# Masks in four row tiles of 32, one transpose for the one-hots of both sides, and later sequences' rows in the MLP's memory

## The chip, the cores and the metric

The kernel runs on one core of one Trainium2 chip. A core has TensorE (matrix products, out of SBUF into PSUM), VectorE, ScalarE and GpSimd (element-wise work), and SyncE, which here issues most of the DMAs. Each engine works through its own list of instructions in order and waits for others by semaphores. The metric is the device time of one execution in microseconds, as the median of several runs.

## What is computed

The kernel joins a clustered attention and an MLP with a layer norm in front. Queries and keys are each assigned to the centroid that they are most similar to; a query attends only to keys of its own cluster.

```
B, H, S, D = 4, 8, 768, 64;  16 centroids per head
q_assign = argmax(q_n @ c_n^T);  k_assign = argmax(k_n @ c_n^T)
mask   = q_assign[:, None] == k_assign[None, :]
attn   = softmax(where(mask, q k^T / 8, -1e9));  a = attn @ v        # per batch and head
x      = a of all heads side by side                                 # (4, 768, 512)
xn     = (x - mean) / sqrt(var + 1e-6) * g
out    = x + relu(xn @ w1) @ w2                                      # w1 512x2048, w2 2048x512
```

## The kernel before

**Pairs, steps, units.** Two heads of one sequence make a pair; there are 16 pairs, four to a sequence (b). Head j of a pair lies in partitions 64j to 64j+63. A step `(n, g, c)` is pair n, half g of its queries (384 columns), block c of its keys (128), for both heads, so a pair has 12 steps. The main loop (L565) takes two steps per turn: a turn is called a unit here, and `slot` 0 to 5 counts the six units of a pair. 

**Scores.** `scores(i)` (L321) fills the PSUM tile `s_ps` of step i (two banks, one per head; two such tiles exist) and takes its exponential. For each head there is first a mask product and then the product of keys and queries, accumulated on it. The mask product multiplies one-hot rows of the queries' clusters (bf16, tile `m` of side 0) with the keys' one-hot rows, turned into 0 for a hit and -2^100 for a miss (`m` of side 1); one head's one-hots fill 16 of its 64 rows, the others are zero. Both products work on 64 rows, head 0 in the upper half of the array and head 1 in the lower (L339). ScalarE then writes `e = exp(s/8)` (L332), with five buffers.

**Weighing.** `weigh(i)` (L344) multiplies `e` with v into `a_ps` (L351; one buffer; each head takes 64 columns of the array) and lets VectorE add up the `e` of a half (L365, L368) for the denominators. After six blocks ScalarE copies the accumulator out (L377).

**Preparing the next pair.** During pair n the next one is prepared, spread over the slots: q and k are transposed on TensorE (`prep_transpose`, L237, k in slot 0 and q of the pair after in slot 5), similarities with the centroids (`prep_sims`, slot 1), their transposes and the maximum (`prep_turn`, `prep_route`, slot 2), and in slot 4 `prep_onehot` (L291): for each side six transposes of one-hots (two heads x 64 columns to 128 rows) into a PSUM tile `oh_ps`, and one ScalarE operation from there into `m`: a copy for the queries (L307), an Identity with bias and scale for the keys (L305). `finish` (L381) computes the denominators of the last pair (slot 1), their reciprocals (slot 3), and scales and stores x (slot 5), once transposed to `xT_d` and once by rows to `x_d`. VectorE also turns the weights, which arrive as float64, into float32 (`split_weight`, `join_weight`).

**The norm.** For a sequence b, `rows_load` (L444) brings rows of x back (tile `xr`, two buffers, from the pool `small`, which lives through the whole kernel), `norm_rows` takes their statistics (`bn_stats`, L455), `norm_stats` (L458) takes the root on ScalarE (L462, with a load of another function table, and the table of the exponential is loaded again at its next use), and `norm_stat_rows` and `norm_apply` spread and apply them.

**The MLP.** After the attention, its pools are closed (L625) and `hid` and `ffn` are opened in their memory. Both layers use a scheme of seven block products instead of eight (`first_layer`, `second_layer`), with sums of operands made by VectorE and copies out of PSUM by ScalarE.

**What sets the order.** In the attention (L547) TensorE, VectorE and ScalarE follow the order that the code writes. In the MLP (L784) only TensorE does; the others, and SyncE throughout, are put in order by a planner, which may place work as soon as its data and memory allow by its own reckoning. The norm of sequence 0 is written into the attention (L529 to L540). That of the others is written into the MLP's loop (L810 to L835), but the planner placed the rows and the statistics of sequences 1 and 2 earlier: the roots (L462) of the four sequences ran at 231.65, 269.82, 353.29 and 506.42 us of the span, and the attention ends near 395.

**The start.** Pair 0's q is loaded in four DMAs on SyncE's queue and its k in four on ScalarE's, behind the centroids (L88, L102). Its products of the first two steps run ahead of the masks, which are then added on top.

Of the kernel before, what the change touches and what calls it, by code (L numbers as in the profile page):

```python
# [19 lines left out]
def kernel(  # L20
# [24 lines left out]
    SCALE = 1.0 / D ** 0.5  # L45
    FAR = 2.0 ** 100
# [5 lines left out]
    small = ctx.enter_context(tc.tile_pool(name="small", bufs=2))  # L52
# [17 lines left out]
    def ps(name, dt=F32, n=512):  # L70
        return pools["t"].tile([P, n], dt, tag="t", name=name)
# [4 lines left out]
    def load(n, names):  # L76
        if n >= len(pairs):
            return
        b, pr = pairs[n]
        for name in names:  # L80

            shape = [P, 2, NT, D] if name == "v" else [P, NT, 2, D]
            t = loads.tile(
                shape, F32, tag=name, name=f"{name}_sb", bufs=2 if name == "v" else 1
            )

            parts = 1 if n or name == "v" else NHALF
            queue = nc.sync if n or name != "k" else nc.scalar  # L88
            for g in range(parts):
                cs = slice(g * NT // parts, (g + 1) * NT // parts)  # L90
                for j in range(2):
                    queue.dma_start(
                        out=t[:, j] if name == "v" else t[:, cs, j, :],
                        in_={"q": q, "k": k, "v": v}[name][b, 2 * pr + j].rearrange(
                            "(p c) d -> p c d", p=P
                        )[:, cs, :],
                    )
            loaded[n][name] = t


    c_sb = const.tile([H * NCL, D], F32, name="c_sb")
    nc.scalar.dma_start(out=c_sb, in_=centroids.rearrange("h c d -> (h c) d"))  # L102
    load(0, "qkv")

    ident = const.tile([P, P], F32, name="ident")
    make_identity(nc, ident)
    identb = const.tile([P, P], BF16, name="identb")
# [6 lines left out]
    eps = const.tile([P, 1], F32, name="eps")  # L114
    nc.gpsimd.memset(eps, 1e-6)

    onehot = route.tile([P, TH, 2, NHALF, 2, D], BF16, name="onehot")
    nc.gpsimd.memset(onehot, 0.0)
    NG = TH * 2 * NHALF * 2
    hits = const.tile([P, B * NPAIR], F32, name="hits")  # L120
    far = const.tile([P, 1], F32, name="far")
    nc.gpsimd.memset(far, -FAR)
# [124 lines left out]
    def prep_sims(n):  # L247

        _, pr = pairs[n]
        sim = ps("sim_ps")  # L250
        for side in range(2):
            for g in range(NHALF):
                r = (side * NHALF + g) * Q
                nc.tensor.matmul(  # L254
                    sim[r : r + Q, :HC],
                    cT[:, pr, :, :].rearrange("p j c -> p (j c)"),
                    prepared[n][side][:, g * HC : (g + 1) * HC],
                    start=True,
                    stop=True,
                    tile_position=(0, r),  # L260
                )
        sim_sb = route.tile([P, HC], F32, tag="sim", name="sim_sb")
        nc.scalar.copy(sim_sb, sim[:, :HC])
        prepared[n]["sim"] = sim_sb
# [10 lines left out]
    def prep_route(n):  # L275
        simT = prepared[n]["simT"]
        sims = simT[:, :HC].rearrange("p (g c) -> p g c", c=NCL)
        best = route.tile([P, NG], F32, tag="best", name="best")
        nc.vector.tensor_reduce(best, sims, AX.X, ALU.max)

        nc.vector.scalar_tensor_tensor(
            out=onehot.rearrange("p c s g j d -> p (c s g j) d")[:, :, :NCL],
            in0=sims,
            scalar=1.0,
            in1=best.unsqueeze(2).to_broadcast([P, NG, NCL]),
            op0=ALU.mult,
            op1=ALU.is_equal,
            accum_out=hits[:, n : n + 1],
        )

    def prep_onehot(n):  # L291
        for side in range(2):
            t = ps("oh_ps", BF16, 1024)
            for g in range(NHALF):
                for c in range(TH):
                    o = (g * TH + c) * P
                    nc.tensor.transpose(  # L297
                        t[:, o : o + P],
                        onehot[:, c, side, g, :, :].rearrange("p j d -> p (j d)"),
                        identb,  # L300
                    )
            m = heads.tile([P, S], BF16, tag=f"m{side}", name=f"m{side}")

            if side:
                nc.scalar.activation(m, t[:, :S], AF.Identity, bias=far, scale=FAR)  # L305
            else:
                nc.scalar.copy(m, t[:, :S])  # L307
            prepared[n]["m", side] = m

# [1 line left out]

    x_d = [spill.tile([NT, P, DM], F32, name=f"x_d{b}") for b in range(B)]
    xs = {}
    soft = {}
    sums = {}
    accs = {}
    late = {}

    def scores(i, first="mask", parts=("mask", "qk", "exp")):  # L321
        n, g, c = steps[i]
        st = prepared[n]
        if parts[0] == first:
            st["s", i] = ps_s.tile([P, 2, 512], F32, tag="s", name="s_ps")
        s = st["s", i]
        keys, cols = slice(c * P, (c + 1) * P), slice(g * HC, (g + 1) * HC)
        rows = [slice(j * D, (j + 1) * D) for j in range(2)]
        for part in parts:
            if part == "exp":  # L330
                e = attn.tile([P, 2, HC], F32, tag="e", name="e", bufs=5)
                nc.scalar.activation(e, s[:, :, :HC], AF.Exp, scale=SCALE)  # L332
                soft[i] = e
                continue
            of_keys, of_queries = {
                "mask": lambda: (st["m", 1], st["m", 0]), "qk": lambda: (st[1], st[0])
            }[part]()
            for j in range(2):
                nc.tensor.matmul(  # L339
                    s[:, j, :HC], of_keys[rows[j], keys], of_queries[rows[j], cols],  # L340
                    start=part == first, stop=part != first, skip_group_check=True,
                )

    def weigh(i):  # L344
        n, g, c = steps[i]
# [97 lines left out]

    def rows_load(b, t):  # L444
        if t < NT:
            x = small.tile([P, DM], F32, tag="xr", name="xr")
            nc.sync.dma_start(out=x, in_=x_d[b][t])
            rows[b, t] = x

# [97 lines left out]
    with tc.manual_schedule(engines=order):  # L547
        prep_transpose(0, 0)
        load(1, "q")
        turn_centroids()  # L550
        prep_transpose(0, 1)
        load(1, "k")
        prep_sims(0)
        scores(0, "qk", ("qk",))
        prep_turn(0)
        scores(1, "qk", ("qk",))
        prep_route(0)
        prep_transpose(1, 0)
        load(2, "q")
        load_weight(0)  # L560
        load_weight(1)
        prep_onehot(0)
        scores(0, "qk", ("mask", "exp"))
        scores(1, "qk", ("mask", "exp"))
        for u in range(len(pairs) * slots):  # L565
            n, slot = divmod(u, slots)
            nxt = n + 1 < len(pairs)
            if slot == 1:
                load(n + 1, "v")
            if slot == 0 and nxt:  # L570
                prep_transpose(n + 1, 1)
                load(n + 2, "k")
            if slot == 1 and nxt:
                prep_sims(n + 1)
            if slot == 2 and nxt:
                prep_turn(n + 1)
                prep_route(n + 1)
            if slot == 4 and nxt:
                prep_onehot(n + 1)
            if slot == 5 and n + 2 < len(pairs):  # L580
                prep_transpose(n + 2, 0)
                load(n + 3, "q")
            if slot == 1 and n:
                finish(n - 1, 0)
            for i in (2 * u + 2, 2 * u + 3):
                if i < len(steps):
                    scores(i)
            weigh(2 * u)
            weigh(2 * u + 1)
            if slot == 3 and n:  # L590
                finish(n - 1, 1)
            if slot == 5 and n:
                finish(n - 1, 2)
            m = 2 * n + slot // 3
            if slot % 3 == 0:
                split_weight(m)
            elif slot % 3 == 1:
                join_weight(m)
                load_weight(m + 2)
            for job in extra.pop((n, slot), ()):  # L600
                job()
# [434 lines left out]
```

## Time and profile before

| | us |
|---|---|
| median of 4 runs (982.78 to 987.36) | 983.2 |
| profiled execution, whole time | 985.0 |
| profiled execution, span from first to last instruction | 983.2 |
| attention, to the last weighing's end | about 395 |
| MLP | about 588 |
| TensorE matmul busy | 961.6 |
| VectorE busy | 642.5 |
| ScalarE busy | 307.7 |

How to read the profile's lines. A group line names the source line, the engine, the operation, what it writes and reads, the tile of TensorE's array that it uses (rows*columns), partitions x elements and type, then the count, the busy time in total, the mean time of one in ns, and the engine's idle time just before with what ended it. A line of the timeline begins with the start and the length of a merged group in us; a bracket gives the idle time before it and what ended that. A line of the waits gives the total, the number and the longest. Matmuls are pipelined: the lengths of two that follow each other overlap, so what an instruction costs on the path is read from one start to the next. A float32 product appears as two passes, each with a record of its own.

### The profile page before, as it was taken

How to read it: one execution, taken by the hardware profiler on the slowest of the kernel's cores; microseconds unless marked ns; L12 is line 12 of the kernel's file. 1: busy time of each engine (PE TensorE's matmuls, PEld its weight loads, DVE VectorE, ACT ScalarE, POOL GpSimd, SP SyncE). 2: the span in 40 equal slices, each digit the busy share in tenths (PEclk: the TensorE clock that was granted, in tenths of full speed). 3: DMA queues.
4: the chain of work that ended last, by engine and by line, in shares of the span. 5: the costliest groups of instructions: out<-in, count | busy, mean ns of one | idle time of the engine just before them, and what ended most of it. 6: DMA issues, size and time to landing. Idle time of an engine off the chain costs nothing.

```text
span 983.2 us, 12870 instructions
## 1 busy us (share of the span) xinstructions
PE 961.6 (98%) x4854; PEld 596.3 (61%) x4854; DVE 642.5 (65%) x1206; ACT 307.7 (31%) x497; POOL 2.8 (0%) x27
## 2 busy tenths in 40 slices
PE   6999999999989989999999999999999999999997
PEld 3444444444444434555888656888556888556886
DVE  3888888998889989776645355654455654455431
ACT  4656666667566655221000121000221000221000
POOL 1000000000000000000000000000000000000000
PEclk9999999999999989999999999999999999999999
DMA  6356666666755643220212000211000212000011
GB/s 173 92 140 168 176 172 164 163 166 170 198 134 142 179 132 87 71 80 17 92 54 71 10 1 1 97 60 64 6 1 0 97 60 70 1 0 6 28 41 37
DMA packets 141444, 84.01 MB, mean 85 GB/s; under 512 B 110608, under 2 KB 127040, under 8 KB 141376
## 3 DMA queue, kind: packets, MB, share of 16 engines
q1 hardware_dynamic: 139104, 82.70, 30.2%
q8 instruction: 40, 0.66, 0.3%
q10 hardware_dynamic: 2272, 0.43, 0.2%
q14 instruction: 28, 0.23, 0.1%
HBM read 64.00 MB, written 19.00 MB: 84 GB/s over the span
## 4 chain that ended last, share of the span: by engine, by line
PE 91%; DVE 5%; DMA 1%; ACT 1%; issue 1%; SPq 0%; ACTq 0%; DVEq 0%
PE x_ps L719 17%; PE x_ps L634 17%; PE s_ps L339 14%; PE a_ps L351 12%; PE z_ps L719 8%; PE z_ps L634 8%; PE y_ps L719 4%; PE y_ps L634 4%; PE qk_ps L237 2%; DVE es L368 2%; PE sim_ps L254 1%; PE den_ps L388 1%; PE oh_ps L297 1%; DVE bn L455 1%; PE simT_ps L270 1%; DMA q_sb<-in_q_dram 1%
## 5 line engine op out<-in xcount | busy, mean ns | idle before, releaser
L332 ACT ACTIVATE e<-s_ps 128x768 f32<-128x768 f32 x192 | 151.6, 813 | 61.1 <-PE s_ps L339 59.4
L339 PE MATMUL s_ps<-t,t 64*128 64x384 f32 x768 | 156.4, 486 | 0.0
L351 PE MATMUL a_ps<-e,v_sb 128*64 128x384 f32 x768 | 146.9, 505 | 3.0 <-ACT x L377 3.0
L368 DVE TENSOR_TENSOR es<-es,e 128x768 f32<-128x768 f32 x128 | 122.1, 954 | 12.1 <-ACT e L332 5.9
L351 PEld LDWEIGHTS a_ps<-e,v_sb 128*64 128x64 f32 x768 | 47.2, 137 | 91.0 <-issue 87.2
L719 PE MATMUL x_ps<-w2t,h 128*128 128x256 f32 x384 | 84.5, 379 | 0.0
L339 PEld LDWEIGHTS s_ps<-t,t 64*128 64x128 f32 x768 | 69.3, 191 | 22.4 <-issue 22.4
L719 PEld LDWEIGHTS x_ps<-w2t,h 128*128 128x128 f32 x384 | 72.7, 190 | 10.1
L649 ACT COPY u<-x_ps 128x384 f32<-128x384 f32 x64 | 30.7, 479 | 135.4 <-PE x_ps L634 135.4
L339 PE MATMUL s_ps<-m,m 64*128 64x384 bf16 x384 | 63.8, 329 | 3.8 <-ACT e L332 2.4
L521 DVE TENSOR_TENSOR ws<-w 128x256 f32<-128x256 f32 x64 | 24.9, 420 | 60.8 <-PE z_ps L634 60.8
L649 ACT COPY p<-x_ps 128x384 f32<-128x384 f32 x32 | 15.3, 479 | 139.9 <-PE x_ps L634 139.0
L730 DVE TENSOR_TENSOR o_sb<-x_ps,xb 128x256 f32<-128x256 f32 x48 | 20.2, 421 | 57.7 <-PE x_ps L719 57.7
L654 DVE TENSOR_TENSOR h<-z_ps,u 128x384 f32<-128x384 f32 x64 | 35.3, 552 | 25.8 <-ACT u L649 14.4
L339 PEld LDWEIGHTS <-m 64*128 64x128 bf16 x384 | 18.7, 93 | 48.2 <-issue 31.2
L634 PE MATMUL x_ps<-xt,ws 128*128 128x384 f32 x128 | 46.6, 487 | 0.9 <-DVE ws L521 0.9
L634 PE MATMUL x_ps<-xn,w 128*128 128x384 f32 x128 | 46.6, 487 | 0.6 <-ACT late L377 0.6
L634 PE MATMUL z_ps<-xt,ws 128*128 128x384 f32 x128 | 46.6, 487 | 0.0
L634 PE MATMUL x_ps<-xt,w 128*128 128x384 f32 x128 | 46.6, 487 | 0.0
L634 PE MATMUL x_ps<-xn,ws 128*128 128x384 f32 x128 | 46.5, 486 | 0.0
L634 PE MATMUL y_ps<-xn,w 128*128 128x384 f32 x128 | 46.5, 486 | 0.0
L634 PE MATMUL z_ps<-xn,ws 128*128 128x384 f32 x128 | 46.5, 486 | 0.0
(122 smaller groups left out, 1296.1 us busy)
## 6 DMA issues: line engine op xcount, KB each, us to landing
raw<-in_moe_w_ch_dram SPq DMA_DIRECT2D x32, 512.0 KB, 3.9
v_sb<-in_v_dram SPq DMA_DIRECT2D x32, 192.0 KB, 3.7
xn<-xT_d SPq DMA_DIRECT2D x16, 384.0 KB, 4.6
xr<-x_d SPq DMA_DIRECT2D x24, 256.0 KB, 2.9
xb<-x_d SPq DMA_DIRECT2D x48, 128.0 KB, 2.1
out_dram<-o_sb SPq DMA_DIRECT2D x48, 128.0 KB, 1.7
q_sb<-in_q_dram SPq DMA_DIRECT2D x30, 192.0 KB, 3.9
k_sb<-in_k_dram SPq DMA_DIRECT2D x30, 192.0 KB, 3.7
```

Of the source, the lines that this page charges most:

```text
L237: nc.tensor.transpose(t[:, c * P : (c + 1) * P], src[:, g * TH + c, :, :].rearrange("p h d -> p (h d)"), ident,)
L254: nc.tensor.matmul(sim[r : r + Q, :HC], cT[:, pr, :, :].rearrange("p j c -> p (j c)"), prepared[n][side][:, g * HC : (g + 1) * HC], start= ...
L332: nc.scalar.activation(e, s[:, :, :HC], AF.Exp, scale=SCALE)
L339: nc.tensor.matmul(s[:, j, :HC], of_keys[rows[j], keys], of_queries[rows[j], cols], start=part == first, stop=part != first, skip_group_ch ...
L351: nc.tensor.matmul(acc[j * D : (j + 1) * D, :HC], loaded[n]["v"][:, j, c, :], e[:, j, :], start=(c == 0), stop=(c == NT - 1),)
L368: nc.vector.tensor_tensor(es, es, soft.pop(i), ALU.add)
L521: nc.vector.tensor_tensor(t[:, i], x, y, op)
L634: nc.tensor.matmul(bank[:, :HC], lhs[:, c, :], rhs[:, c, :], start=first and c == 0, stop=c == NDH - 1, skip_group_check=True,)
L649: nc.scalar.copy(t, bank[:, :HC])
L654: nc.vector.tensor_tensor(h, bank[:, :HC], other, ALU.add)
L719: nc.tensor.matmul(bank[:, :MH], hidden[lhs + (c,)][:, tt * P : (tt + 1) * P], rhs[:, c, :], start=first and c == 0, stop=c == NFH - 1, sk ...
L730: nc.vector.tensor_tensor(o, bank[:, :MH], x, ALU.add)
```

## The change

- **Masks of a unit together.** `masks(u)` issues four mask products, for two steps and two heads, each on 32 rows at row 0, 32, 64 and 96 of the array. The keys' one-hots of even blocks lie in rows 0 to 63 and of odd blocks in rows 64 to 127 (`mk`); the queries' one-hots lie in both halves (`mq`). Then come the products and exponentials of the two steps (`products`, `exponentials`).
- **One-hots of both sides in one transpose.** A one-hot has 32 columns instead of 64, so two sides and two heads fill 128 columns, and six transposes do for what took twelve. Four ScalarE operations on 64 partitions each (two Identities over 384 elements, two copies over 768) fill `mk` and `mq` in place of two on 128 partitions over 768.
- **Rows in other memory.** `xr` comes from `last` for sequence 0, and from `ffn`, which exists only after the attention, for the others.
- **First loads.** q of pair 0 is issued ahead of the centroids, and of q and k the first head's DMAs go to SyncE's queue and the second head's to ScalarE's.

```diff
-            queue = nc.sync if n or name != "k" else nc.scalar
             for g in range(parts):
                 cs = slice(g * NT // parts, (g + 1) * NT // parts)
                 for j in range(2):
+                    queue = nc.scalar if parts > 1 and j else nc.sync
                     queue.dma_start(
...
+    load(0, "q")
     c_sb = const.tile([H * NCL, D], F32, name="c_sb")
     nc.scalar.dma_start(out=c_sb, in_=centroids.rearrange("h c d -> (h c) d"))
-    load(0, "qkv")
+    load(0, "kv")
...
-    onehot = route.tile([P, TH, 2, NHALF, 2, D], BF16, name="onehot")
+    onehot = route.tile([P, TH, NHALF, 2, 2, Q], BF16, name="onehot")
...
-                r = (side * NHALF + g) * Q
+                r = (g * 2 + side) * Q
...
     def prep_onehot(n):
-        for side in range(2):
-            t = ps("oh_ps", BF16, 1024)
-            for g in range(NHALF):
-                for c in range(TH):
-                    o = (g * TH + c) * P
-                    nc.tensor.transpose(
-                        t[:, o : o + P],
-                        onehot[:, c, side, g, :, :].rearrange("p j d -> p (j d)"),
-                        identb,
-                    )
-            m = heads.tile([P, S], BF16, tag=f"m{side}", name=f"m{side}")
-            if side:
-                nc.scalar.activation(m, t[:, :S], AF.Identity, bias=far, scale=FAR)
-            else:
-                nc.scalar.copy(m, t[:, :S])
+        t = ps("oh_ps", BF16, 1024)
+        for g in range(NHALF):
+            for c in range(TH):
+                o = (g * TH + c) * P
+                nc.tensor.transpose(
+                    t[:, o : o + P],
+                    onehot[:, c, g, :, :, :].rearrange("p s j d -> p (s j d)"),
+                    identb,
+                )
+        mq = heads.tile([P, S], BF16, tag="mq", name="mq")
+        mk = heads.tile([P, NT // 2, P], BF16, tag="mk", name="mk")
+        keys = t[D:P, :S].rearrange("p (c two m) -> p c two m", two=2, m=P)
+        for i in range(2):
+            rows = slice(i * D, (i + 1) * D)
+            nc.scalar.activation(mk[rows], keys[:, :, i, :], AF.Identity, bias=far[:D], scale=FAR)
+            nc.scalar.copy(mq[rows], t[:D, :S])
...
+    def masks(u, first=True):
+        n, g, c = steps[2 * u]
+        mk, mq = prepared[n]["m"]
+        for i in range(2):
+            for j in range(2):
+                rows = slice(i * D + j * Q, i * D + (j + 1) * Q)
+                nc.tensor.matmul(
+                    score[2 * u + i][:, j, :HC],
+                    mk[rows, c // 2, :],
+                    mq[rows, g * HC : (g + 1) * HC],
+                    start=first, stop=not first, skip_group_check=True,
+                    tile_position=(rows.start, 0),
+                )
...
+    def scores(u):
+        score_tiles(u)
+        masks(u)
+        for i in (2 * u, 2 * u + 1):
+            products(i)
+            exponentials(i)
...
-            x = small.tile([P, DM], F32, tag="xr", name="xr")
+            x = (ffn if b else last).tile([P, DM], F32, tag="xr", name="xr", bufs=2)
...
-            for i in (2 * u + 2, 2 * u + 3):
-                if i < len(steps):
-                    scores(i)
+            if 2 * u + 2 < len(steps):
+                scores(u + 1)
             weigh(2 * u)
             weigh(2 * u + 1)
```

In the built program the changes of order are these: ScalarE's list has the roots of sequences 1 and 2 after the MLP's first copies instead of between the one-hot copies and exponentials of pairs 10 and 13; VectorE's list has their twelve `bn_stats` between the additions of the first layer of sequence 0; SyncE's list has their twelve loads behind the first three to four `xb` loads of sequence 0, among the last pair's stores and ahead of the fifth `xb` load and of `xn` of sequence 1. TensorE's list has, per unit, four masks and then the eight passes of the products.

More of the change, by code (lines that the diff above doesn't have):

```diff
@@ L115 @@
     nc.gpsimd.memset(eps, 1e-6)
-    onehot = route.tile([P, TH, 2, NHALF, 2, D], BF16, name="onehot")
+    onehot = route.tile([P, TH, NHALF, 2, 2, Q], BF16, name="onehot")
     nc.gpsimd.memset(onehot, 0.0)
-    NG = TH * 2 * NHALF * 2
+    NG = TH * NHALF * 2 * 2
     hits = const.tile([P, B * NPAIR], F32, name="hits")
@@ L281, in prep_route @@
         nc.vector.scalar_tensor_tensor(
-            out=onehot.rearrange("p c s g j d -> p (c s g j) d")[:, :, :NCL],
+            out=onehot.rearrange("p c g s j d -> p (c g s j) d")[:, :, :NCL],
             in0=sims,
@@ L291, in prep_onehot @@
     def prep_onehot(n):
-        for side in range(2):
-            t = ps("oh_ps", BF16, 1024)
-            for g in range(NHALF):
-                for c in range(TH):
-                    o = (g * TH + c) * P
-                    nc.tensor.transpose(
-                        t[:, o : o + P],
-                        onehot[:, c, side, g, :, :].rearrange("p j d -> p (j d)"),
-                        identb,
-                    )
-            m = heads.tile([P, S], BF16, tag=f"m{side}", name=f"m{side}")
-            if side:
-                nc.scalar.activation(m, t[:, :S], AF.Identity, bias=far, scale=FAR)
-            else:
-                nc.scalar.copy(m, t[:, :S])
-            prepared[n]["m", side] = m
+        t = ps("oh_ps", BF16, 1024)
[14 more added lines that the diff above has]
+            nc.scalar.copy(mq[rows], t[:D, :S])
+        prepared[n]["m"] = mk, mq
     xT_d = [spill.tile([NDC, P, S], F32, name=f"xT_d{b}") for b in range(B)]
@@ L315 @@
     xs = {}
+    score = {}
     soft = {}
@@ L319 @@
     late = {}
-    def scores(i, first="mask", parts=("mask", "qk", "exp")):
+    def masks(u, first=True):
[11 more added lines that the diff above has]
+                )
@@ L322, in scores, with products @@
+    def products(i, first=False):
         n, g, c = steps[i]
         st = prepared[n]
[L324 to L342, printed above, removed]
+        for j in range(2):
+            rows = slice(j * D, (j + 1) * D)
+            nc.tensor.matmul(
+                score[i][:, j, :HC],
+                st[1][rows, c * P : (c + 1) * P],
+                st[0][rows, g * HC : (g + 1) * HC],
+                start=first, stop=not first, skip_group_check=True,
+            )
@@ L344, in weigh, with exponentials, score_tiles @@
+    def exponentials(i):
+        e = attn.tile([P, 2, HC], F32, tag="e", name="e", bufs=5)
+        nc.scalar.activation(e, score.pop(i)[:, :, :HC], AF.Exp, scale=SCALE)
+        soft[i] = e
+    def score_tiles(u):
+        for i in (2 * u, 2 * u + 1):
+            score[i] = ps_s.tile([P, 2, 512], F32, tag="s", name="s_ps")
+    def scores(u):
+        score_tiles(u)
+        masks(u)
+        for i in (2 * u, 2 * u + 1):
+            products(i)
+            exponentials(i)
     def weigh(i):
@@ L553 @@
         prep_sims(0)
-        scores(0, "qk", ("qk",))
+        score_tiles(0)
+        products(0, True)
         prep_turn(0)
-        scores(1, "qk", ("qk",))
+        products(1, True)
         prep_route(0)
@@ L562 @@
         prep_onehot(0)
-        scores(0, "qk", ("mask", "exp"))
-        scores(1, "qk", ("mask", "exp"))
+        masks(0, False)
+        exponentials(0)
+        exponentials(1)
         for u in range(len(pairs) * slots):
```

## The prediction

> **What bounds the kernel now.** I read the page first: TensorE is busy for almost the whole span and is nearly all of the chain that ended last, so a change counts where it changes TensorE's own time or makes TensorE wait.
>
> ```profile
> span 983.2 us, 12870 instructions
> PE 961.6 (98%) x4854; PEld 596.3 (61%) x4854; DVE 642.5 (65%) x1206; ACT 307.7 (31%) x497; POOL 2.8 (0%) x27
> PE 91%; DVE 5%; DMA 1%; ACT 1%; issue 1%; SPq 0%; ACTq 0%; DVEq 0%
> L339 PE MATMUL s_ps<-m,m 64*128 64x384 bf16 x384 | 63.8, 329 | 3.8 <-ACT e L332 2.4 <-ACT m L305 1.4
> ```
>
> The masks have 63.8 us of busy time, but busy matmuls overlap; their share of the path has to come from start times. Second, TensorE's waits. Few, and two of them (2.4, with 0.8 just before it, and 3.0) lie far inside the attention:
>
> ```profile
> PE a_ps L351 <- ACT x L377: 3.0, 1, 3.0
> PE s_ps L339 <- ACT e L332: 2.4, 1, 2.4
> PE s_ps L339 <- ACT m L305: 1.4, 1, 1.4
> PE qk_ps L237 <- ACT m L307: 0.8, 1, 0.8
> ```
>
> Third, the timeline around the first of them: ScalarE, then TensorE.
>
> ```profile
> 265.11 1.28 ACT L462 ACT_TABLE_LOAD   x1
> 269.82 0.30 ACT L462 ACTIVATE stat<-mv,eps 128x6 f32<-128x6 f32 x1 [3.43 <-DVE mv L456]
> ...
> 271.62 1.28 ACT L332 ACT_TABLE_LOAD   x1
> ```
>
> ```profile
> 273.78 0.34 PE L339 MATMUL s_ps<-m,m 64*128 64x384 bf16 x2 [2.38 <-ACT e L332]
> ...
> 274.90 1.52 PE L339 MATMUL s_ps<-t,t 64*128 64x384 f32 x4
> ```
>
> This is norm_stats of sequence 1. Its rows were loaded and its stats queued in the middle of the attention, ScalarE stood 3.43 us for the last row's mean, loaded two tables of 1.28, and the one-hot copies and exponentials queued behind it came late. After the wait four products take 1.52 instead of 0.81 (granted clock 0.93 over 260 to 283, 1.00 over 53 to 76): an idle of 3 us also cost clock. Sequence 2 does the same at 348 to 360.
>
> Fourth, one undisturbed unit of two steps, and the start-up, where the products follow an instruction of another tile size:
>
> ```profile
> 52.97 0.34 PE L339 MATMUL s_ps<-m,m 64*128 64x384 bf16 x2
> 53.14 0.81 PE L339 MATMUL s_ps<-t,t 64*128 64x384 f32 x4
> 53.79 0.33 PE L339 MATMUL s_ps<-m,m 64*128 64x384 bf16 x2
> 53.95 0.81 PE L339 MATMUL s_ps<-t,t 64*128 64x384 f32 x4
> 54.69 1.51 PE L351 MATMUL a_ps<-e,v_sb 128*64 128x384 f32 x8
> 56.13 0.84 PE L297 MATMUL oh_ps<-identb,onehot 128*128 128x128 bf16 x12
> 56.91 0.34 PE L339 MATMUL s_ps<-m,m 64*128 64x384 bf16 x2
> ```
>
> ```profile
> 12.30 0.55 PE L270 MATMUL simT_ps<-ident,sim_sb 128*128 128x128 f32 x3
> 12.78 0.92 PE L339 MATMUL s_ps<-t,t 64*128 64x384 f32 x4
> ```
>
> ```profile
> 13.20 0.49 PE L339 MATMUL s_ps<-t,t 64*128 64x384 f32 x2
> ```
>
> Read the starts. The two masks of a step already run side by side: 0.16 to 0.17 for the pair. Products of one step: 0.65 (53.14 to 53.79) when masks of the same tile shape follow, 0.74 when the 128x64 weighing follows: 0.09 for the change of tile shape. Every change in the trace costs this, also one of the row size alone: twelve transposes of 128 rows take 0.78 up to the 64-row masks, 0.057 each and again 0.10. After a change the first pass of products is longer too: 12.78 to 13.20 is 0.42, against 0.32 within a shape, since its weights (183 ns) are loaded only when the shape is set; in a plain unit they load beside the masks.
>
> **The change, part by part.**
>
> 1. *Rows of later sequences in MLP memory.* In the changed program's order, norm_stats of sequences 1 and 2 leave the attention and stand among the MLP's copies; their 12 bn_stats stand in VectorE's first layer of sequence 0. What goes: from the starts of the first weighing, pair 10 takes 28.34 us and pairs 2 to 8 take 23.26: 5.08. The second stall makes the last unit of pair 13 7.07 instead of 3.97 and the first of pair 14 7.39 instead of 4.59: 5.90. **-11.0**. Next late there would be the score buffers, which in other units are free 0.4 us or more ahead. What it brings: 12 x (0.68 + 0.17) = 10.2 us of VectorE into 405 to 470 us, where it is busy for 46.9 of 65.0: 57.1 of 65, so it fits on average. SP gets 12 more loads there, ahead of the fifth xb load and of xn; neither is used before the second layer. Each load waits for one of two buffers, then lands in 2.9 us, and additions queue behind a bn_stats that waits. Bounds: 0, and 6 waits of 2.9 - 0.85 = 2.05 (two buffers in flight), 12.3. TensorE has eight banks and some 9 us per hidden block, so I take the near end, **0**. ScalarE's stats wait likewise, before one bank's copy each.
>
> 2. *One transpose for both sides.* 12 to 6 per pair, on the path: 16 x 6 x 0.057 = **-5.5**.
>
> 3. *Masks of two steps together.* Per unit one mask pair goes, -0.16. But 32-row tiles stand between 128-row weighing and 64-row products, so one more shape change, +0.095, and the products' weights no longer load ahead, +0.10. Net +0.035; over 95 units **+3.3**. No 32-row tile is in the trace. Lower bound: neither cost, -0.16 x 95 = -15.2. Upper: the four run two at a time, 0.16 more per unit, +18.5. Nearest are the row-size changes of 128 to 64, which all paid, and the four 32-column tiles of sim_ps and den_ps, which start 7 ns apart and finish eight passes in 0.67: so I take +3.3.
> The third and fourth mask now wait for the second exponential of the last unit, and all products queue behind them. In a plain unit the second exponential ends 0.93 us after the weighing starts (54.00 + 1.62 against 54.69), and the weighing takes 1.44; as the first exponential starts later now, I count 1.0: cover 0.4.
>
> The Trainium skill (TensorEngine Tiling, Key Properties) speaks against this part: changing the tiling mode, not merely the tile, drains the engine, and it lists 32x128 and 64x128 as different modes. The 0.09 rows agree. TensorE: Matmul & The Clock Gate (Part 3) has four 32-row tiles at 3.07 times one, not 4; as an estimate that page would add 0.05 per unit, 4.6 us, and no run here shows it.
>
> 4. *Four one-hot copies instead of two.* Before, 0.80 and 0.91 us, 1.49 from first start to next work. Now twice a half-width Identity and a full-width copy on 64 partitions. By elements per partition: 0.69 for a copy, 0.38 (half-width t copies, two in 0.86) to 0.49 for the Identity: 2.3, +0.8. Bounds: partitions halve the cost, 1.1; no overlap at all, 2.8. In slot 4, from the first transpose: copies begin at 0.55, end at 2.85, exponentials end at 2.85 + 0.70 + 0.81 = 4.36. TensorE reaches the next masks at 4.75 (56.13 to 60.88) - 0.34 + 0.035 = 4.45: cover 0.1, cost **0** for 14 pairs; upper 0.4 x 14 = 5.6, lower 0. Pair 14 has no transposes of 0.81 there: **+0.8** once. At start-up the masks wait for these copies already (1.4): **+0.8**, and up to 1.7 more if the longer idle costs clock, as 3.0 us did and 1.4 did not.
>
> 5. *First loads on both queues, q ahead of the centroids.* The q transposes waited (4.31, 6.49), but the k transposes at 7.59 waited for ScalarE's copy, behind tables and roots. Bounds -1 and +1 (the 1.3 us wait for q); **0**, as the later link stays.
>
> Sum: -11.0 - 5.5 + 3.3 + 0.8 + 0.8 = -11.6. The profiled execution took 985.0 (span 983.2, 1.8 around it): 973.4. The median of the runs is 1.8 lower, so 971.6: **972**.
>
> **Rivals.**
> - *A, 32- and 64-row tiles switch freely.* Part 3 becomes -15.2, TensorE arrives 0.4 earlier in slot 5 and waits 0.3 x 14 = 4.2 there: 972 - 18.5 + 4.2 = **958**. For it: no 32-row row in the trace. Against: each change of shape there paid.
> - *B, the four masks do not run together.* Two at a time adds 15.4: **987**, slower than before; one at a time adds 46. It decides from 0.12 us per unit. Against: the concurrent pairs and quartets.
> - *C, the copies are slower than their element counts.* +5.6 in slot 5: **978**.
> - *D, the stall moves instead of going*: bn_stats behind 2.9 us loads hold up the MLP's additions, about the bound of part 1, +11: **983**. For it: VectorE at 88% and two buffers. Against: the six such loads that before ran there (435 to 445) made no wait of TensorE.
>
> **How the numbers follow.** Forecast 0.63, A 0.12, C 0.10, D 0.08, B 0.07. The range takes in A and C and most of the open costs, and leaves out B and D: 958 to 981. A measurement tells about 0.5%, 4.9 us: faster 0.83 (forecast, A, C, less their tails), same 0.11 (D, B at two at a time in part, tails), slower 0.06.
>
> **What would show it.** Pairs of even length, about 23.2 us, with no wait of TensorE on ScalarE near 270 and 350 and full clock; a unit with four masks and then products 0.26 later, the first pass 0.42, a unit 3.20 instead of 3.16; six transposes at 0.057; ScalarE's stats after 400 us. Wrong would be: a first pass of 0.32 (A), masks 0.16 apart (B), a wait of the third mask in slot 5 in every pair (C), or waits of the first layer on VectorE (D).

## The result and the profile after

The changed kernel takes 984.15 us in the median, the kernel before 983.41 us: a ratio of 1.0008, with a 95% interval from 1.0001 to 1.0015. So it is about 0.1% slower. The forecast was 972 us, with a range of 958 to 981, and it gave "the same" a chance of 0.11. The profiled execution took 984.13 us (before: 985.0), its span is 982.4 us (before: 983.2).

The page of the changed kernel, the same four lines as were shown of before:

```profile
span 982.4 us, 12707 instructions
PE 962.9 (98%) x4758; PEld 589.0 (60%) x4758; DVE 641.9 (65%) x1206; ACT 315.1 (32%) x525; POOL 2.2 (0%) x27
PE 83%; DVE 7%; ACT 6%; issue 2%; DMA 1%; SPq 1%; ACTq 0%; DVEq 0%
L331 PE MATMUL s_ps<-mq,mk 32*128 32x384 bf16 x384 | 38.3, 333 | 5.6 <-ACT mq L310 2.8
```

TensorE is as busy as before (98%). The line to look at is the third, the shares of the chain that ended last: TensorE's share fell from 91% to 83%, ScalarE's rose from 1% to 6%. Somewhere TensorE now waits for ScalarE again and again.

The stalls that the change was to remove are gone. The stretches of the trace, us and length first, then busy time of TensorE, its weight loads, VectorE, ScalarE and GpSimd, the granted clock, DMA share and GB/s, in the kernel before:

```profile
260.00:283.00 23.00, 19.85 (x128) 9.03 (x128) 19.24 (x31) 14.75 (x21) 0.00 (x0) 0.93 0.62 163
340.00:363.00 23.00, 19.97 (x125) 8.40 (x122) 20.01 (x37) 13.45 (x20) 0.00 (x0) 0.85 0.52 138
405.00:470.00 65.00, 65.00 (x207) 38.86 (x206) 46.92 (x121) 13.51 (x28) 0.00 (x0) 1.00 0.18 51
```

and in the changed kernel:

```profile
260.00:283.00 23.00, 22.86 (x155) 9.69 (x153) 19.80 (x30) 15.27 (x24) 0.00 (x0) 1.00 0.68 177
340.00:363.00 23.00, 22.86 (x155) 9.88 (x153) 20.83 (x33) 14.68 (x25) 0.00 (x0) 1.00 0.44 117
405.00:470.00 65.00, 65.00 (x208) 39.09 (x207) 52.56 (x148) 14.82 (x30) 0.00 (x0) 1.00 0.35 99
```

From 260 to 283 us TensorE is busy for 22.86 us (before: 19.85) at a clock of 1.00 (before: 0.93). But a pair now takes 23.66 us between the start of its first weighing and the next pair's (pairs 1 to 13; pair 9 takes 23.76), where an undisturbed pair before took 23.26. The timeline of TensorE in pair 1: its first weighing, then from a plain unit into the last slot, and the first weighing of pair 2:

```profile
47.49 1.51 PE L374 MATMUL a_ps<-e,v_sb 128*64 128x384 f32 x8
...
57.25 0.34 PE L331 MATMUL s_ps<-mq,mk 32*128 32x384 bf16 x4
57.52 1.56 PE L344 MATMUL s_ps<-t,t 64*128 64x384 f32 x8
59.01 1.51 PE L374 MATMUL a_ps<-e,v_sb 128*64 128x384 f32 x8
60.45 0.51 PE L297 MATMUL oh_ps<-identb,onehot 128*128 128x128 bf16 x6
60.89 0.34 PE L331 MATMUL s_ps<-mq,mk 32*128 32x384 bf16 x4
61.16 1.56 PE L344 MATMUL s_ps<-t,t 64*128 64x384 f32 x8
62.65 1.51 PE L374 MATMUL a_ps<-e,v_sb 128*64 128x384 f32 x8
64.10 0.87 PE L238 MATMUL qk_ps<-ident,q_sb 128*128 128x128 f32 x6
64.90 0.81 PE L331 MATMUL s_ps<-mq,mk 32*128 32x384 bf16 x4
65.64 1.24 PE L344 MATMUL s_ps<-t,t 64*128 64x384 f32 x6
...
71.14 1.51 PE L374 MATMUL a_ps<-e,v_sb 128*64 128x384 f32 x8
```

Four masks last 0.34 at 57.25 and at 60.89, but 0.81 at 64.90. The two masks of the first step start there at once, the third starts at 65.375: it waits 0.47. The list of waits does not show this: the first two masks are still running for 0.33 of it, and the idle rest of 0.14 is too short to be listed. What the third mask waits for stands in ScalarE's timeline:

```profile
61.00 0.58 ACT L309 ACTIVATE mk<-oh_ps,far 64x384 bf16<-64x384 bf16 x1 [1.00 <-PE oh_ps L297]
61.60 0.79 ACT L310 COPY mq<-oh_ps 64x768 bf16<-64x768 bf16 x1
62.41 0.58 ACT L309 ACTIVATE mk<-oh_ps,far 64x384 bf16<-64x384 bf16 x1
63.00 0.79 ACT L310 COPY mq<-oh_ps 64x768 bf16<-64x768 bf16 x1
63.81 1.51 ACT L353 ACTIVATE e<-s_ps 128x768 f32<-128x768 f32 x2
```

The four copies start 0.60, 0.81 and 0.59 us after each other and the exponential starts 0.81 after the last: none begins before the one ahead has ended. The two exponentials behind them, on 128 partitions, do overlap: each lasts 0.81 and the two together 1.51. The second one ends at 65.32 and lets the third mask go.

In pair 14, where no q transposes stand ahead of the masks, the first mask waits as well:

```profile
372.33 0.34 PE L331 MATMUL s_ps<-mq,mk 32*128 32x384 bf16 x2 [0.51 <-ACT e L353]
373.03 0.34 PE L331 MATMUL s_ps<-mq,mk 32*128 32x384 bf16 x2 [0.36 <-ACT e L353]
```

The third mask starts 0.70 after the second, and this unit takes 4.48 us from weighing to weighing instead of a plain unit's 3.205: 1.28 in all.

And the start, on TensorE:

```profile
16.44 0.50 PE L297 MATMUL oh_ps<-identb,onehot 128*128 128x128 bf16 x6
18.64 0.34 PE L331 MATMUL s_ps<-mq,mk 32*128 32x384 bf16 x2 [1.71 <-ACT mq L310]
20.06 0.34 PE L331 MATMUL s_ps<-mq,mk 32*128 32x384 bf16 x2 [1.08 <-ACT mq L310]
...
22.19 2.36 PE L344 MATMUL s_ps<-t,t 64*128 64x384 f32 x8
24.48 1.51 PE L374 MATMUL a_ps<-e,v_sb 128*64 128x384 f32 x8
```

The first weighing starts at 24.48 (before: 20.68). TensorE stands idle for 1.71 and 1.08 us for the copies, and the eight passes that take 1.56 in a plain unit take 2.36: the granted clock is 0.50 from 20.42 to 23.82.

```profile
20.42:23.82 3.40, 3.40 (x16) 2.14 (x18) 2.21 (x4) 1.92 (x4) 0.00 (x0) 0.50 0.11 25
```

Where the time went, from one profiled execution to the other:

| | us |
|---|---|
| stalls of pairs 10, 13 and 14 gone | -11.0 |
| masks: plain unit 3.205 instead of 3.16, 94 units | +4.2 |
| six transposes (0.44) instead of twelve (0.78), 15 pairs | -5.1 |
| masks wait for the exponential: 0.47 in 14 pairs, 1.28 in pair 14 | +7.8 |
| start, to the first weighing: 24.48 instead of 20.68 | +3.8 |
| MLP, from the last weighing's end: 587.9 instead of 588.5 | -0.6 |
| sum | -0.9 |
| measured, 984.13 - 985.0 | -0.9 |

### The profile page after: what moved, and what is told of

It reads as the page before. It is cut to its first block, busy times and chain, and to the rows that moved or that the text cites. A ratio compares the mean times of both kernels' runs of the same rounds, so it can differ in the third digit from the quotient of the medians.

```text
span 982.4 us, 12707 instructions
## 1 busy us (share of the span) xinstructions
PE 962.9 (98%) x4758; PEld 589.0 (60%) x4758; DVE 641.9 (65%) x1206; ACT 315.1 (32%) x525; POOL 2.2 (0%) x27
## 4 chain that ended last, share of the span: by engine, by line
PE 83%; DVE 7%; ACT 6%; issue 2%; DMA 1%; SPq 1%; ACTq 0%; DVEq 0%
PE x_ps L743 17%; PE x_ps L658 17%; PE s_ps L344 9%; PE a_ps L374 9%; PE z_ps L743 8%; PE z_ps L658 8%; PE y_ps L743 4%; PE y_ps L658 4%; DVE es L391 3%; ACT e L353 2%; ACT mq L310 2%; PE s_ps L331 2%; PE qk_ps L238 1%; PE sim_ps L255 1%; DMA q_sb<-in_q_dram 1%
## 5 line engine op out<-in xcount | busy, mean ns | idle before, releaser
L353 ACT ACTIVATE e<-s_ps 128x768 f32<-128x768 f32 x192 | 145.2, 808 | 76.3 <-PE s_ps L344 75.2
L344 PE MATMUL s_ps<-t,t 64*128 64x384 f32 x768 | 151.6, 513 | 0.0
L374 PE MATMUL a_ps<-e,v_sb 128*64 128x384 f32 x768 | 144.8, 499 | 0.0
L391 DVE TENSOR_TENSOR es<-es,e 128x768 f32<-128x768 f32 x128 | 122.4, 956 | 15.6 <-ACT e L353 9.0
L344 PEld LDWEIGHTS s_ps<-t,t 64*128 64x128 f32 x768 | 66.7, 188 | 42.8 <-issue 18.6
L727 DVE TENSOR_TENSOR w2t<-w 128x512 f32<-128x512 f32 x32 | 20.2, 685 | 36.8 <-PE z_ps L743 36.8
L331 PE MATMUL s_ps<-mq,mk 32*128 32x384 bf16 x384 | 38.3, 333 | 5.6 <-ACT mq L310 2.8
```

The costliest lines, as they stand in the source:

```text
L331: nc.tensor.matmul(score[2 * u + i][:, j, :HC], mk[rows, c // 2, :], mq[rows, g * HC : (g + 1) * HC], start=first, stop=not first, skip_gr ...
L344: nc.tensor.matmul(score[i][:, j, :HC], st[1][rows, c * P : (c + 1) * P], st[0][rows, g * HC : (g + 1) * HC], start=first, stop=not first, ...
L353: nc.scalar.activation(e, score.pop(i)[:, :, :HC], AF.Exp, scale=SCALE)
L374: nc.tensor.matmul(acc[j * D : (j + 1) * D, :HC], loaded[n]["v"][:, j, c, :], e[:, j, :], start=(c == 0), stop=(c == NT - 1),)
L391: nc.vector.tensor_tensor(es, es, soft.pop(i), ALU.add)
L727: nc.vector.tensor_tensor(o[:, c : c + 2], x[:, c : c + 2], y[:, c : c + 2], ALU.subtract)
```

## The experiments

### Part 1 alone, in the kernel before

```diff
-            x = small.tile([P, DM], F32, tag="xr", name="xr")
+            x = (ffn if b else last).tile([P, DM], F32, tag="xr", name="xr", bufs=2)
```

> The kernel before with part 1 alone (rows of later sequences in MLP memory). My theory: the two stalls of the attention (5.1 and 5.9 us in the profiled execution) go and nothing comes in their place, since in the changed kernel the MLP took 588.5 us against 589.0: 972 to 975 us, every pair 23.26 us, no wait of TensorE on ScalarE near 270 and 350. Rival 1, the stall moves into the MLP once the attention is shorter: 980 to 984. Rival 2, the rows are worth less in an ordinary execution than in the profiled one because its clock loss was by chance: 976 to 979.

Measured: 974.28 us against 982.78 of the kernel before beside it, a ratio of 0.9921 (0.99 to 0.9942). Repeated on another chip, beside the later experiments:

> Part 1 alone once more, on the same chip as the kernel with parted copies and mended start, to set the two side by side: 974.3 us as measured.

There it is 973.76 against 982.56, 0.991 (0.9894 to 0.9927). The place of the first stall, on TensorE, in the kernel with part 1 alone:

```profile
264.34 1.51 PE L351 MATMUL a_ps<-e,v_sb 128*64 128x384 f32 x8
265.79 0.84 PE L297 MATMUL oh_ps<-identb,onehot 128*128 128x128 bf16 x12
...
269.72 0.88 PE L237 MATMUL qk_ps<-ident,q_sb 128*128 128x128 f32 x6
270.53 0.34 PE L339 MATMUL s_ps<-m,m 64*128 64x384 bf16 x2
```

The masks follow the q transposes at once; before, they waited 2.38 us there. Pairs 1 to 13 take 23.26 (pair 9: 23.36), the first weighing starts at 20.86, and TensorE's share of the chain that ended last is 97%. The span fell by 10.8 (983.2 to 972.4), as the stalls read from the trace said (11.0). By the medians it is 8.5 and 8.8: the one profiled execution of before, 985.0, lies some 2 us above the medians of its runs (982.6 to 983.4). This one line is faster than both kernels, so the rest of the change cost what this part gained: the span of the changed kernel is 9.9 longer (982.35 and 972.43), and the rows above give +7.8 (waits of the masks), +3.6 (start), +4.2 (masks), -5.1 (transposes) and -0.6 (MLP), together +9.9.

### Part 1 undone in the changed kernel

```diff
-            x = (ffn if b else last).tile([P, DM], F32, tag="xr", name="xr", bufs=2)
+            x = small.tile([P, DM], F32, tag="xr", name="xr")
```

> The changed kernel with part 1 undone (rows from the old pool). Theory: the other parts together cost what part 1 brings, so the stalls come back on top of them: 992 to 996 us, with two late units near pairs 10 and 13. Rival, the new masks leave ScalarE or the scores enough room to hide the stall in part: 985 to 989.

Measured: 995.6 us, 1.0136 (1.0113 to 1.0159) times the kernel before, 11.4 over the changed kernel. The stall of pair 10, on TensorE:

```profile
281.72 0.50 PE L331 MATMUL s_ps<-mq,mk 32*128 32x384 bf16 x2 [3.97 <-ACT e L353]
...
282.85 2.93 PE L344 MATMUL s_ps<-t,t 64*128 64x384 f32 x8
```

It waits 3.97 us, and the eight passes take 2.93 instead of 1.56, at half the clock. By the spans the part is worth 11.4 here and 10.8 alone, so the others do not take away its gain: what was lost stands in them by itself.

### The copies spread over two slots

In the changed kernel the transposes and the two copies of the lower half go to slot 3, the two of the upper half to slot 4. Nothing is added or taken away.

```diff
...
-            if slot == 4 and nxt:
+            if slot == 3 and nxt:
                 prep_onehot(n + 1)
+                copy_onehot(n + 1, 0)
+            if slot == 4 and nxt:
+                copy_onehot(n + 1, 1)
```

> The changed kernel with the four one-hot copies parted: transposes and the copies of the lower half in slot 3, those of the upper half in slot 4. Theory: the 0.47 us that the third mask waits in slot 5 of every pair is the copies' 2.81 us ahead of the exponentials; with 1.4 us in front of two units each it goes, and pairs take 23.19 us instead of 23.66: 984 - 6.9 = 976.5 to 978. Rival, the wait is the price of needing both score buffers at once, whatever ScalarE has done before: the wait stays near 0.4 or moves to slot 4, 982 to 985.

Measured: 977.61 us, 0.9951 (0.9933 to 0.9968) times the kernel before, and 6.5 less than the changed kernel. The last slot of a pair, on TensorE:

```profile
109.14 1.51 PE L376 MATMUL a_ps<-e,v_sb 128*64 128x384 f32 x8
110.58 0.88 PE L238 MATMUL qk_ps<-ident,q_sb 128*128 128x128 f32 x6
111.38 0.34 PE L333 MATMUL s_ps<-mq,mk 32*128 32x384 bf16 x4
```

The four masks are back at 0.34, and TensorE's share of the chain is 97%, as with part 1 alone. A pair takes 23.19, that is 0.07 less than in the kernel before: the transposes' -0.34 and the masks' +0.27 (6 x 0.045), which in this arrangement can be read undisturbed. So the queue of copies ahead of the exponentials is what cost 0.47 in each pair. What stays over the kernel with part 1 alone, 3.3 us, is the start: the first weighing is at 24.89 instead of 20.86, 4.0 later, of which the pairs give back about 1.0 (15 x 0.07); the rest lies in the last pair and the MLP. The clock is at half from 18.4 to 25.2.

### The old first loads

The changed kernel with the queues and the order of the first loads as they were before.

```diff
+            queue = nc.sync if n or name != "k" else nc.scalar
...
-                    queue = nc.scalar if parts > 1 and j else nc.sync
...
-    load(0, "q")
...
-    load(0, "kv")
+    load(0, "qkv")
```

> The changed kernel with the first loads as before (centroids first, q on SyncE's queue, k on ScalarE's). Theory: the centroids landed at 5.28 instead of 2.83 us because q's packets were ahead of them, and the whole start up to the one-hots came 1.0 us later; undone, the first weighing starts 1.0 us earlier, 983 us, and the half clock of 20.4 to 23.8 us stays, as it comes from the idle for the copies. Rival, the late full clock (13.6 instead of 11.75 us) and the half clock both come from the new load order: first weighing 2.5 us or more earlier, 981.5.

Measured: 983.57 us, 1.0015 (1.0005 to 1.0026) times the kernel before; the spans differ by 0.6 (981.8 and 982.4). On TensorE:

```profile
14.81 0.50 PE L296 MATMUL oh_ps<-identb,onehot 128*128 128x128 bf16 x6
...
23.64 2.00 PE L373 MATMUL a_ps<-e,v_sb 128*64 128x384 f32 x8
```

The one-hots are ready 1.6 us earlier than after the change (14.81, 16.44), but only half of it reaches the first weighing (23.64, 24.48). The clock is at half from 17.8 to 24.7, twice as long as in the changed kernel, and that takes the other half back. In the profiled execution after the change the centroids had arrived at 5.28 (before: 2.83), behind q, and the transposes of k began at 8.45 (before: 7.59). The new order of loads makes the one-hots later: their transposes start between 14.6 and 15.6 us in the profiles with the old loads, between 15.8 and 16.5 in those with the new ones. In the whole time the two cannot be told apart: the intervals of 1.0015 and 1.0008 overlap.

### Masks grouped, on 64 rows

Part 1 alone, and the masks of both steps of a unit ahead of the products as in part 3, but on 64 rows as before: no new tile shape.

```diff
-            for i in (2 * u + 2, 2 * u + 3):
-                if i < len(steps):
-                    scores(i)
+            ahead = [i for i in (2 * u + 2, 2 * u + 3) if i < len(steps)]
+            for i in ahead:
+                scores(i, parts=("mask",))
+            for i in ahead:
+                scores(i, parts=("qk", "exp"))
```

> Part 1 alone (974.3 us), and the masks of a unit put together as in the change, but on 64 rows as before. Theory: it is the third tile shape that makes a unit of the changed kernel 3.205 us instead of 3.16, not the grouping; here masks and products share a shape, so the unit is 3.16, the first pass of products 0.32, and the time 973.5 to 975.5. Rival: grouping itself costs, as the third mask waits for the second exponential of the unit before: units over 3.2 us or a wait in slot 5, 978 or more.

Measured: 974.67 us, 0.9919 (0.99 to 0.9938). TensorE in a plain unit:

```profile
54.32 0.50 PE L339 MATMUL s_ps<-m,m 64*128 64x384 bf16 x4
54.65 1.45 PE L339 MATMUL s_ps<-t,t 64*128 64x384 f32 x8
56.04 1.51 PE L351 MATMUL a_ps<-e,v_sb 128*64 128x384 f32 x8
57.48 0.84 PE L297 MATMUL oh_ps<-identb,onehot 128*128 128x128 bf16 x12
```

From the masks' start to the transposes' it is 3.16, as in the kernel before, against 3.20 to 3.205 with the 32-row tiles. The masks take 0.33 up to the products instead of 0.27, and the products 1.39 up to the weighing instead of 1.49. So in a unit the order costs nothing, and what the four masks on 32 rows save up to the products (0.06) is less than what the products behind another tile shape lose (0.10). The whole time is still 0.9 over part 1 alone on the same chip (973.76): the first weighing starts at 21.82 instead of 20.73, with a half clock from 18.9 to 22.3. The Trainium skill (TensorEngine Tiling, Key Properties) says that changing the tiling mode drains the array, and these rows agree: 0.10 us of a 3.2 us unit.

### The two whole copies cut in halves

Part 1 alone, twelve transposes and 64-row masks as before, but each of the two copies on 128 partitions cut in two on 64 partitions: four operations of the same length as the two, so only the number of partitions changes.

```diff
...
-            if side:
-                nc.scalar.activation(m, t[:, :S], AF.Identity, bias=far, scale=FAR)
-            else:
-                nc.scalar.copy(m, t[:, :S])
+            turned.append(t)
...
+        for i in range(2):
+            rows = slice(i * D, (i + 1) * D)
+            nc.scalar.copy(prepared[n]["m", 0][rows], turned[0][rows, :S])
+            nc.scalar.activation(
+                prepared[n]["m", 1][rows], turned[1][rows, :S], AF.Identity,
+                bias=far[rows], scale=FAR,
+            )
```

> Part 1 alone, and the two one-hot copies of 128 partitions cut into four of 64, in the order lower copy, lower Identity, upper copy, upper Identity (768 elements each). It asks why the four copies of the changed kernel did not overlap (0.60, 0.81, 0.59, 0.81 us from start to start). Theory 1, ScalarE overlaps one operation's end with the next one's start only if their first partitions are the same: from start to start 0.69 (copy to Identity, same half), 0.93 (to the other half), 0.69, 0.93. Theory 2, operations on 64 partitions never overlap with the next: 0.81, 0.93, 0.81, 0.93. Theory 3, it was the shift between the halves of input and output that did it, and here there is none: 0.69, 0.80, 0.69, 0.80. The time is about 976 in all three, mostly by the start.

Measured: 979.06 us, 0.9962 (0.9949 to 0.9975) times the kernel before, and 5.3 over part 1 alone on the same chip. The expected 976 was missed by 3: pairs take 23.38 instead of 23.26 and pair 14 0.94 more, and the first weighing starts at 23.51 instead of 20.73, with a half clock from 20.5 to 23.9. ScalarE in slot 4:

```profile
83.18 0.79 ACT L308 COPY m<-oh_ps 64x768 bf16<-64x768 bf16 x1 [1.06 <-PE oh_ps L298]
83.98 0.90 ACT L309 ACTIVATE m<-oh_ps,far 64x768 bf16<-64x768 bf16 x1
84.89 0.79 ACT L308 COPY m<-oh_ps 64x768 bf16<-64x768 bf16 x1
85.71 0.90 ACT L309 ACTIVATE m<-oh_ps,far 64x768 bf16<-64x768 bf16 x1
86.63 1.51 ACT L336 ACTIVATE e<-s_ps 128x768 f32<-128x768 f32 x2
```

From start to start 0.81, 0.91, 0.82 and 0.92: an operation on 64 partitions lasts as long as one on 128, and none of these overlaps the next. Over the trace an Identity starts before the copy ahead has ended in 2 of 32 cases, and nothing starts early behind an Identity in 32. Theory 2 of the expectation fits; theories 1 and 3 fall. It is not the whole rule. In the experiment that spread the copies, the lower-half copy and the 128-partition exponential behind it are 0.70 apart though the copy lasts 0.79, in all 15 pairs; in the changed kernel the upper-half copy ahead of the exponential is 0.81 apart. What decides whether the next one may start early stays open.

### Spread copies, old loads, and VectorE for half of the first copies

The kernel with spread copies, with the old first loads, and with pair 0's upper-half copies on VectorE, so that the masks wait less at the start.

```diff
...
+        if n == 0 and i == 1:
+            nc.vector.tensor_scalar(mk[rows], keys[:, :, i, :], FAR, -FAR, op0=ALU.mult, op1=ALU.add)
+            nc.vector.tensor_copy(mq[rows], t[:D, :S])
+            return
```

> The changed kernel with the copies parted over two slots (977.6 us), with the first loads as before, and with pair 0's upper-half copies on VectorE beside ScalarE's lower half. Theory: the masks of pair 0 then start about 1.4 us earlier, TensorE idles about 1.7 us there instead of 2.8, no half clock follows, and the first weighing starts at 21.0 to 21.5 us instead of 24.9: 973.5 to 974.5, level with part 1 alone or up to 1 us better, as pairs take 23.19 us against 23.26. Rival: the half clock near 20 us has another cause than this idle and stays: 976 to 977.

Measured: 975.8 us, 0.9937 (0.9922 to 0.9952), 2.0 over part 1 alone. TensorE at the start:

```profile
17.64 0.34 PE L336 MATMUL s_ps<-mq,mk 32*128 32x384 bf16 x2 [1.71 <-ACT mq L316]
18.62 0.34 PE L336 MATMUL s_ps<-mq,mk 32*128 32x384 bf16 x2 [0.64 <-DVE mq L313]
...
23.04 1.51 PE L379 MATMUL a_ps<-e,v_sb 128*64 128x384 f32 x8
```

The second wait fell from 1.08 to 0.64, and the first weighing starts at 23.04, not at 21.0 to 21.5 as expected: the clock is 0.50 from 19.3 to 22.7, as the rival had it. The idle time for the copies does not decide that alone. The kernel with grouped 64-row masks stood idle for 1.40 (copies) and 0.36 (an exponential) and had a half clock from 18.9 to 22.3; the kernel with part 1 alone had 1.39 and none.

The ten traces show a little more. Counted from when the clock first became full, it changes only on a grid of 3.41 us: stretches at either clock last 3.41, 6.83 or 10.24 us, or more of such steps (262.83 is 77 of them). In the step of this grid that ended where the clock fell, TensorE was idle for 1.68 us or more in every case (2.35 here, 2.71 in the changed kernel, 1.76 with grouped masks); where it stayed full, for 1.83 at most. Part 1 alone stood idle for 1.91 (a load) and 1.39 us (the copies) between 13.0 and 17.9, but for no more than 1.83 in one step, and kept its clock. So where the idle time falls on the grid matters, and not only its sum. What decides between 1.68 and 1.83, and why the half clock lasts one step or two, stays open.

One-hot transposes and 32-row masks with all that was found bring less than part 1 alone.

## Why the prediction was wrong

**Part 1, the rows: right.** Taken at -11.0, the spans gave -10.8 alone and +11.4 when undone. The cost taken for it in the MLP, 0, held: from 405 to 470 us VectorE is busy for 52.6 of 65 (before: 46.9; 57.1 was worked out), and TensorE for 65.0 in both. In the MLP of the changed kernel TensorE's only listed wait for VectorE is 0.15, at 398 us; the kernel before has 0.90 at the same place, about the MLP's -0.6. Rival D falls. (The six loads named against it were issued from 423 us on, not 435; nothing hangs on it.) In medians the part is worth 8.5 to 8.8: the profiled execution of before lay some 2 us above its median, that of the changed kernel lies on it (984.13 and 984.15). So the 1.8 us taken off at the end did not carry over. That they were clock lost behind the stalls, and so counted twice in the sum, fits the granted clock of the runs: it is 0.994 in the profiled execution of before, where, once full, it is at half only behind the two stalls and at the very end. Of the 31 runs beside the experiments the ten at 0.995 or less took 982.7 to 984.8 us, the three at 0.999 or more 979.7 to 980.6, 5.5 to 6.8 over part 1 alone, about the idle time of the stalls without any loss of clock (2.4 + 0.8 + 3.0). No trace of these runs shows where they lost their clock, so it is argued and not shown.

**Part 2, one transpose: right.** -0.34 a pair, as worked out.

**Part 3, the masks: right in mechanism and nearly in size.** Four masks start 3 ns apart, the first products 0.26 to 0.27 later, the first pass takes 0.42, and a unit 3.205 instead of 3.16: +4.2 where +3.3 was forecast. Rivals A and B fall. The estimate from the skill's page on the clock gate (TensorE: Matmul & The Clock Gate, Part 3), 0.05 more per unit on top, is not seen: a unit was forecast without it at 3.195.

**Part 4, the copies: the step that failed.** It put their wait in slot 5 at nothing, and the wait is 0.47 in each of 14 pairs. The prediction took 2.3 us for the four copies, with overlap, between 1.1 and 2.8 "no overlap at all", and a cover of 0.1. They take 2.81. TensorE reached the masks when forecast (4.45 after the transposes' start), the second exponential ended 0.41 after the third mask was due, and the mask started 0.05 later. That is rival C, held at 0.10. The 2.3 was taken by elements per partition from copies that overlap each other; all of those worked on 128 partitions, and no row of the trace of before had a 64-partition copy followed by another. The Trainium skill (ScalarE: Activation LUTs, What ACT_TABLE_LOAD costs) has back-to-back activations overlap by about 93 ns, beside measurements on 128 partitions. The rows on 128 partitions agree (0.11 between exponentials), those on 64 partitions in the changed kernel do not (0.00), and the measurement decides. With no overlap the working gives the measured lateness of the exponential: 0.51 more, less 0.1 of cover, is 0.41. Pair 14, taken at 0.8, cost 1.28, again 0.5 more. Spreading the copies over two slots took the waits away, and cutting whole copies to 64 partitions took their overlap away; both are shown above.

**The start, part 4 and part 5: wrong in size.** +0.8 for the copies and 0 for the loads; measured +3.8. The copies took 1.2 more than before (3.89 from the transposes to the next work, 2.72 before), the loads 1.0 in these two executions (the one-hots at 16.44 instead of 15.43, the bound given was +1; the other profiles of old and new loads lie 0.2 to 1.8 apart), and the half clock 1.6 (the text allowed "up to 1.7 more" and left it out of the sum).

**The sum.** From -11.6: the waits of the masks +7.0 over their 0.8, the start +3.0, the masks' own time +0.9, the transposes +0.4 (15 pairs, the first stands in the start), the MLP -0.6: -0.9, which is what the two profiled executions differ by. And 1.8 for the median. The range left out what happened because it moved one term at a time: C alone made 978. But a copy without overlap, the wait in each pair, the longer start and the half clock behind the longer idle time were not independent: the first brings the second and part of the third, and lengthens the idle time ahead of the fourth.

## What to carry to other kernels

An edit costed at nothing because 0.1 us of cover is left has to be costed at its upper bound: the copies went to half the partitions here, and none got shorter for that. When a change bundles parts, run the one with the plainest evidence alone: one line of memory placement, read from two waits in the trace, made most of the gain, and the rest gave it back. Look at TensorE's share of the chain that ended last, not at its busy share: all kernels here are 97 or 98% busy, while the share of the chain goes from 82% to 98%.

## What was not expected of the hardware

- ScalarE operations on 64 partitions last as long as on 128 (0.79 for 768 elements in both the cut and the changed kernel) and mostly do not overlap: 0.60, 0.81, 0.59 and 0.81 from start to start in the changed kernel, 0.81 to 0.92 when whole copies were cut, against 0.70 between exponentials of 0.81. The exception is a copy to the lower half with an exponential behind it: 0.70 after a copy of 0.79.
- At the start the clock fell to half for one step of 3.41 us (in the changed kernel, with part 1 undone, with grouped masks, with halved copies and with VectorE's help) or two, 6.83 us (with spread copies, with the old loads). The idle time ahead of the masks was between 1.8 and 2.8 us in them, and neither length goes with either end; the kernel before and part 1 alone had 1.4 and no half clock.
- A wait of 0.47 us in 14 pairs is absent from the list of waits, since instructions issued ahead of it were still running for most of it. It can be read only from the starts, or from a merged group that lasts 0.81 instead of 0.34.
